# DeltaNet then Fourier mixing on one core: V scaled a step sooner, query products moved into the series, and the first two tiles of the second sample put in program order on all engines

## The chip, the cores and the metric

The kernel runs on one core of one Trainium2 chip. The metric is the device time of one execution in microseconds (us), lower is better. A core has a matrix engine (PE, whose weight loads the profile lists apart as PEld), a vector engine (DVE), a scalar engine (ACT), a GpSimd engine (POOL), and SP, whose queue issues nearly all DMAs here. Each engine works through its own queue of instructions in order and waits on semaphores for the others.

## The reference

Two blocks follow each other. All arrays are float32 but the two weights, which numpy makes float64.

```python
# q, k, v: (4, 8, 768, 48); beta: (4, 8, 768)
k_n = k / (norm(k) + 1e-6)
for t in range(768):                       # state: (4, 8, 48, 48), from zero
    y[t] = q[t] @ state
    state += beta[t] * outer(k_n[t], v[t] - k_n[t] @ state)
x = y as (4, 768, 384)                     # heads side by side
u = x + real(fft(fft(x, axis=1), axis=2))
un = (u - mean(u)) / sqrt(var(u) + 1e-6)
out = u + relu(un @ w_ch1) @ w_ch2         # 384 -> 1536 -> 384
```

## The kernel before

**Tiles.** A tile ("load") is 128 tokens of one of the 4 samples, all 8 heads; there are 24, numbered g, six to a sample (`NL` = 6). A tile has two chunks of 64 tokens. Four tiles make a round r for one inversion (`RL` = 4), so tiles 6 and 7, the first two of the second sample, are the last of round 1, and tile 8 begins round 2.

**What is made ahead of a tile.** `pre_a` turns K with PE (line 113, evicted by ACT at line 320) and makes the Gram products. `invert16(r)` inverts the diagonal blocks of a round with some 60 small DVE instructions, handed out in 46 steps: a transposition of G (line 475), a square root on ACT (481), eleven steps on norms, 30 steps of forward substitution (517 and 520), and two transpositions back (523, 526). `pre_q` turns Q (line 538, evicted at 320), multiplies it with K (548) and masks the product on DVE (555). `pre_m16(g)` joins the blocks of the inverse: Z on ACT (608), a product and its evictions (614, 617, 624), three products in a row evicted at 645 (DVE), 647 (ACT) and 649 (DVE), and V scaled by the norms (629), on DVE for the tiles before 8. For the first sample it also makes W and U (668, 670, evicted at 671 and 672). Each `yield` in such a generator ends a step, and the main program hands the steps out one by one.

**The recurrence.** `step(g, c)` carries the state over one chunk: a product with the state, a subtraction on DVE (720 for the first sample, 698 after it), for later samples a product with the inverse evicted on ACT (708), a product with K and an addition to the state (737 or 739). `outputs(g)` makes two products, evicted at 762 and 772/774.

**Weights.** The float64 weights come as pairs of int32 and are converted to float32 by `weight`, piece by piece, 12 pieces for each weight. One piece costs three ACT instructions (277, 278, 285) and five on DVE (286, 288, then 292, 295, 299). The generator of it, `conv`, gives two steps a piece: the second half of one piece, and the first half of the next. Line 256 then issues the DMA of a later piece.

**Stages.** The first sample's recurrence is the "series", a loop over g (lines 1175 to 1253). Then come the folds and sums of the Fourier block, then the loop over `KF` = 12 chunks of the first MLP with keys of tiles 9 to 11, `pre_m16(7)` and `conv` between them (lines 1301 to 1307). Then `period(g, side)` follows for every tile from 6 on. It has six slots (the loop at line 1059); each slot hands out pieces of the recurrence, of the inversion `inv`, of `conv` (tile 6 only), and of the MLP of the sample before (`side`): turned activations (`ptr`, evicted at 922), `ph` products evicted into hT at 936, and `po` products.

**Order.** Within `tc.manual_schedule(engines=...)` the engines named issue in the order of the program text; the order of the other engines is chosen by the framework's scheduler. Before the change there are three such regions: the first, up to line 1312, for PE, DVE, ACT and POOL; the second (1313 to 1316: the rest of `pre_q(6)`, and tiles 6 and 7) for PE alone; the third, from tile 8 on, for the four engines again. In the second region the scheduler places what DVE, ACT and POOL do, also among instructions of its neighbours. SP's order is the scheduler's everywhere.

**Buffers.** PSUM has three tags with two buffers each: `pair` (state products, query products, W), `one` (turned tiles, products of `pre_m16`, V with the inverse) and `post` (`ph`, `ptr`, `po`). A product waits until the buffer of the last but one of its tag was read.

Of the kernel before, what the change touches and what calls it, by code (L numbers as in the profile page):

```python
# [20 lines left out]
RL = 4  # L21
# [43 lines left out]
def kernel(  # L65
# [14 lines left out]
    NL = S // L  # L80
# [517 lines left out]
    def pre_m16(g):  # L598


        r, li = divmod(g, RL)
        K, GU = Ks[g % 3], GXs.pop((g, 16))
        MTd, Md, nT = rounds[r]
        m8 = slice(8 * li, 8 * li + 8)
        tags = ("QT", "LQ") if g < 2 * RL else ("WT", "WT")
        Z = wk.tile([128, 8, 2, W], F32, tag=tags[0], bufs=2, name="Z")
        for e in range(2):
            nc.scalar.activation(Z[:, :, e, :], Md[:, m8, :], ACT.Copy, scale=m_blk[:, e:e + 1])
        if g != 2 * RL:
            yield  # L610
        px = ps_one()
        for m in range(8):
            for hh in range(2):
                mm(px[full[hh], C * m:C * m + C], GU[full[hh], m, :],
                   Z[full[hh], m].rearrange("p b t -> p (b t)"), m == 0)
        ND2 = wk.tile([128, 8, C], F32, tag=tags[1], bufs=2, name="ND")
        nc.scalar.activation(ND2.rearrange("p m t -> p (m t)"), px, ACT.Copy)
        MT = wk.tile([128, 8, 2, W], F32, tag="MT", bufs=2, name="MT")
        for e in range(2):
            if g == 0:  # L620
                nc.vector.tensor_scalar(MT[:, :, e, :], MTd[:, m8, :], m_blk[:, e:e + 1], None,
                                        op0=ALU.mult)
            else:
                nc.scalar.activation(MT[:, :, e, :], MTd[:, m8, :], ACT.Copy,  # L624
                                     scale=m_blk[:, e:e + 1])

        def scaled_v():
            V = Vs.pop(g)
            (nc.vector if g < 2 * RL else nc.gpsimd).tensor_tensor(
                V.rearrange("p c j d -> p (c j) d"), V.rearrange("p c j d -> p (c j) d"),  # L630
                nT[:, m8, None].broadcast_to([128, 8, D]), op=ALU.mult)
            return V

        V = None if g else scaled_v()
        flat = "p m b t -> p (m b t)"
        yield
        for i in range(3):
            pz = ps_one()
            src = Z if i == 1 else MT
            for m in range(8):  # L640
                for hh in range(2):
                    mm(pz[full[hh], C * m:C * m + C], ND2[full[hh], m, :],
                       src[full[hh], m].rearrange("p b t -> p (b t)"), m == 0)
            if i == 0:
                nc.vector.tensor_tensor(Z.rearrange(flat), MT.rearrange(flat), pz, op=ALU.subtract)  # L645
            elif i == 1:
                nc.scalar.activation(MT.rearrange(flat), pz, ACT.Copy)  # L647
            else:
                nc.vector.tensor_tensor(MT.rearrange(flat), Z.rearrange(flat), pz, op=ALU.add)
            if i < 2 or g < 2 * RL:  # L650
                yield
        V = V or scaled_v()
        if g >= NL:
            pre[g] = (K, MT, V)
            yield
            return
        yield
        WT = wk.tile([128, 2, 2, 2, C], F32, tag="WT", bufs=2, name="WT")
        U0 = wk.tile([128, 2, 4, D], F32, tag="U0", bufs=2, name="U0")
        pw = ps_pair()  # L660
        pu = ps_one()
        for c in range(2):
            for j in range(4):
                for hh in range(2):
                    mt = MT[full[hh], 4 * c + j].rearrange("p b t -> p (b t)")
                    jj, jp = divmod(j, 2)
                    o = (2 * c + jj) * C
                    mm(pw[full[jp], hh, o:o + C], K[full[hh], 4 * c + j, :], mt, c == 0 and jj == 0)
                    o = (4 * c + j) * D
                    mm(pu[full[hh], o:o + D], mt, V[full[hh], c, j, :], c == 0 and j == 0)  # L670
        nc.scalar.activation(U0.rearrange("p c j d -> p (c j d)"), pu[:, 0:8 * D], ACT.Copy)
        nc.scalar.activation(WT.rearrange("p h c j t -> p h (c j t)"), pw[:, :, 0:4 * C],
                             ACT.Copy)
        pre[g] = (K, WT)
        Us[g] = U0
        yield
# [333 lines left out]
    def period(g, side):  # L1010
# [48 lines left out]
        for i in range(SLOTS):  # L1059
            if i == (2 if r + 1 < R16 else 3) and fresh and inv:  # L1060
                drain(inv)
                inv = None
            for p in pieces[i]:
                advance(p)
            if i == 5 and n + 1 == NL:
                o = outputs(g)
                drain(o)
                late = None
            if li == 1 and i == 1 and r > 1 and not last_round:
                inv = invert(r + 1)  # L1070
            if g == NL:
                advance(inv, 5)
                advance(conv, 2 if i < 5 else 4)
            elif inv:
                advance(inv, 8 if r + 1 < R16 else 6)
            if n + 2 >= NL and 0 < i < 5:

                if n + 2 == NL and i == 1:
                    fold = folds(b)
                advance(fold, 2)  # L1080
            at = SLOTS * n + i + 1
            if b > 1:
                want = 2 + (PIECES - KEEP - 2) * at // (SLOTS * NL)
            else:

                want = 2 + KF + (2 + 2 * KF) * at // (2 * SLOTS)
                if n > 1:
                    want = 4 + 3 * KF + (PIECES - KEEP - 4 - 3 * KF) * (at - 2 * SLOTS) // (
                        SLOTS * (NL - 2))
            for p in behind[i]:  # L1090
                advance(p)
            advance(side, want - done)
            done = max(want, done)
        load_v(g + 2)

    engines = {mybir.EngineType.PE, mybir.EngineType.DVE, mybir.EngineType.Activation,
               mybir.EngineType.Pool}
    with tc.manual_schedule(engines=engines):
# [76 lines left out]
        for g in range(NL - 1):  # L1175
# [4 lines left out]
            if g == 0:  # L1180
                advance(c0)
                fill(5)
                advance(nm)
                advance(n2)
                advance(c1)
                fill(5)
                advance(nm)
                advance(n2)
                advance(c1)
                fill(5)  # L1190
                advance(nm)
                advance(n2)
                drain(nm)
                advance(n2)
                drain(qs[1])
                advance(qs[2])
                advance(ms[3])
            else:
                advance(c0)
                if g == 2:  # L1200
                    advance(n2)
                else:
                    fill(5)
                if g > 2:
                    convert(1)
                advance(nm)
                advance(late)
                advance(c0)

                fill(5)  # L1210
                if g == 2:
                    convert(1)
                advance(n2)
                drain(late)
                if g == 4:
                    fold = folds(0)
                    fd = part(fold, 8)
                    advance(keys[0])
                advance(nm)
                advance(c1)  # L1220
                fill(4 if g == 1 else 3)
                if g > 1 and g != 4:
                    convert(2)
                drain(nm)
                advance(n2)
                advance(c1)
                if g == 4:
                    convert(2)
                    advance(n2)
                    drain(qs[g + 1])  # L1230
                    convert(1)
                else:
                    fill(1)
                    if g > 1:
                        convert(1)
                    advance(n2)
                    if g > 1:
                        convert(g - 1)
                    drain(qs[g + 1])
                if g + 2 < NL:  # L1240
                    advance(qs[g + 2])
                if g > 1 and g < 4:
                    advance(ms[g + 3])
            late = outputs(g)
# [10 lines left out]
        g = NL - 1  # L1255
# [54 lines left out]
            drain(m)  # L1310
        done = 3 + KF
        inv = invert16(2)
    with tc.manual_schedule(engines={mybir.EngineType.PE}):
        drain(nq)
        for g in range(NL, NL + 2):
            period(g, side)
    with tc.manual_schedule(engines=engines):
        for b in range(1, B):
            for g in range(max(NL * b, NL + 2), NL * (b + 1)):
                period(g, side)  # L1320

            advance(side, KEEP - 12)
# [42 lines left out]
```

## Time and profile before

| | |
|---|---|
| times of three runs | 743.04 us median, 741.8 to 745.75 |
| the profiled execution | 743.66 us, of which the span is 741.9 us |
| PE busy | 689.6 us, 93% of the span |
| DVE busy | 377.1 us, 51% |
| ACT busy | 262.5 us, 35% |
| POOL busy | 79.1 us, 11% |
| mean granted clock of PE | 0.972 |

Start times below are microseconds from the start of the span. The stages lie as follows: the series from about 40 to 113, the Fourier block to about 128, the first MLP loop from there to 160, tiles 6 and 7 from 160 to about 217. A line of the timeline reads: start, duration of the run of equal instructions, engine, source line, operation, what it writes and reads, count, and in brackets how long the engine was idle before it and what ended that. The products in float32 are recorded as two instructions each, so "x6" of `ph` is one chunk of three products.

### The profile page before, as it was taken

To read this page: it belongs to the slowest core of one execution; us is meant where nothing else is said; L and a number is where in the kernel's file an instruction comes from. 1 tells how busy PE (TensorE), PEld (TensorE's weight loads), DVE (VectorE), ACT (ScalarE), POOL (GpSimd) and SP (SyncE) were. 2 spreads that over 40 slices of the span, in tenths; PEclk is the share of its full clock that TensorE was granted. 3 is DMA by queue.
4 is the path that set the end of the run, shared out by engine and by line. 5 is a ranking of instruction groups with operands and counts; after the bars stand their busy time and mean duration, and the time that the engine had idled before them with its cause. 6 is when DMAs were issued, how large, how long until landed. Compare 5 with 4: busy or idle time off the path is not lost.

```text
span 741.9 us, 23087 instructions
## 1 busy us (share of the span) xinstructions
PE 689.6 (93%) x10176; PEld 529.3 (71%) x10176; DVE 377.1 (51%) x957; ACT 262.5 (35%) x641; POOL 79.1 (11%) x138
## 2 busy tenths in 40 slices
PE   6878789969999978999999999999999999999998
PEld 5667777757667656878768778777677687777684
DVE  5877787798711996170596328288212241600000
ACT  4534774787324212234323243133223121221120
POOL 8000001110000102031101120030112100200000
PEclk8699999988999999999999999999999999999999
DMA  9842452153124211003212211001110000000000
GB/s 153 221 72 43 98 140 87 24 138 99 28 51 83 46 34 28 1 11 72 41 39 50 45 40 28 11 23 37 43 34 13 12 12 5 18 1 21 11 11 21
DMA packets 108791, 36.10 MB, mean 49 GB/s; under 512 B 101873, under 2 KB 105234, under 8 KB 108690
## 3 DMA queue, kind: packets, MB, share of 16 engines
q1 hardware_dynamic: 106866, 33.86, 21.1%
q8 instruction: 80, 1.31, 0.8%
q0 software_dynamic: 640, 0.43, 0.4%
q10 hardware_dynamic: 1184, 0.33, 0.3%
q14 instruction: 21, 0.17, 0.1%
HBM read 29.88 MB, written 4.72 MB: 47 GB/s over the span
## 4 chain that ended last, share of the span: by engine, by line
PE 75%; DVE 15%; ACT 6%; issue 2%; DMA 1%; DVEq 0%; ACTq 0%
PE po L110 24%; PE ph L110 21%; PE one L110 15%; PE pair L110 9%; PE one L113 2%; DVE M L450 1%; DVE tmp L446 1%; PE ptr L113 1%; PE unread L1111 1%; DVE tmp L517 1%; DVE M L520 1%; DMA C<-in_k_dram 1%; DVE Z L645 1%; DVE S L739 1%; DVE w L292 1%
## 5 line engine op out<-in xcount | busy, mean ns | idle before, releaser
L110 PE MATMUL po<-w,hT 128*128 128x384 f32 x576 | 204.8, 495 | 0.0
L110 PE MATMUL ph<-unT,w 128*128 128x256 f32 x828 | 197.2, 390 | 0.0
L110 PEld LDWEIGHTS ph<-unT,w 128*128 128x128 f32 x828 | 155.1, 193 | 23.2
L110 PEld LDWEIGHTS po<-w,hT 128*128 128x128 f32 x576 | 103.5, 190 | 56.4
L936 ACT ACTIVATE hT<-ph 128x256 f32<-128x256 f32 x138 | 52.8, 383 | 144.2 <-PE ph L110 143.3
L951 DVE TENSOR_TENSOR x<-x,po 128x384 f32<-128x384 f32 x24 | 13.2, 551 | 107.0 <-PE po L110 107.0
L739 DVE TENSOR_TENSOR S<-S,pair 128x192 f32<-128x192 f32 x40 | 14.0, 351 | 71.2 <-PE pair L110 71.1
L110 PEld LDWEIGHTS one<-V,MT 64*64 64x64 f32 x768 | 31.1, 143 | 20.0 <-issue 7.7
L882 DVE TENSOR_TENSOR x<-x,one 128x193 f32<-128x193 f32 x24 | 8.5, 355 | 66.5 <-ACT Q L873 66.5
L110 PE MATMUL one<-V,MT 64*64 64x48 f32 x768 | 36.4, 230 | 4.2 <-DVE V L698 2.6
L450 DVE TENSOR_TENSOR M<-M,tmp 128x31 f32<-128x31 f32 (+15 forms) x93 | 34.5, 371 | 3.2
L446 DVE TENSOR_TENSOR tmp<-A,M 128x31 f32<-128x31 f32 (+15 forms) x93 | 34.1, 366 | 2.5
L698 DVE TENSOR_TENSOR V<-V,pair 128x192 f32<-128x192 f32 x33 | 11.5, 349 | 37.6 <-PE pair L110 31.4
L110 PE MATMUL one<-MT,ND 64*64 64x64 f32 x768 | 28.9, 225 | 1.1 <-ACT MT L647 0.7
L110 PEld LDWEIGHTS one<-dtab,F 97*128 97x128 f32 (+1 forms) x192 | 25.1, 191 | 6.4 <-ACT KT L320 1.3
L894 POOL TENSOR_SCALAR rstd<-mv 128x1 f32<-128x1 f32 x24 | 6.6, 276 | 216.4 <-DVE mv L890 216.4
L110 PEld LDWEIGHTS one<-MT,ND 64*64 64x64 f32 x768 | 26.5, 141 | 2.3 <-ACT MT L624 1.1
L320 ACT ACTIVATE QT<-one 128x512 f32<-128x512 f32 x24 | 14.3, 595 | 38.7 <-PE one L113 38.6
L110 PE MATMUL one<-dtab,F 97*128 97x97 f32 (+1 forms) x192 | 26.0, 275 | 0.9 <-ACT KT L320 0.9
L566 POOL TENSOR_TENSOR MT<-A,pack 128x512 f32<-128x512 f32 x12 | 12.8, 1067 | 130.3 <-PE one L110 64.8
L110 PEld LDWEIGHTS pair<-U,K 64*64 64x64 f32 x704 | 15.5, 134 | 15.5 <-issue 13.2
L110 PEld LDWEIGHTS pair<-S,KT 48*64 48x64 f32 x528 | 10.7, 133 | 21.7 <-issue 10.9
(181 smaller groups left out, 1029.4 us busy)
## 6 DMA issues: line engine op xcount, KB each, us to landing
w<-in_moe_w_ch_dram SPq DMA_DIRECT2D x12, 384.0 KB, 7.2
E<-in_moe_w_ch_dram SPq DMA_DIRECT2D x12, 384.0 KB, 3.8
out_dram<-x SPq DMA_DIRECT2D x24, 192.0 KB, 1.9
K<-in_k_dram SPq DMA_DIRECT2D x92, 48.0 KB, 2.3
V<-in_v_dram SPq DMA_DIRECT2D x92, 48.0 KB, 2.3
C<-in_k_dram SPq DMA_DIRECT2D x18, 192.0 KB, 9.5
Q<-in_q_dram SPq DMA_DIRECT2D x18, 192.0 KB, 3.4
w<-in_q_dram SPq DMA_DIRECT2D x6, 192.0 KB, 7.9
```

Of the source, the lines that this page charges most:

```text
L110: nc.tensor.matmul(o, lhsT=lhsT, rhs=rhs, start=start, stop=stop, skip_group_check=True)
L113: nc.tensor.matmul(o, lhsT=src, rhs=ident[0:src.shape[0], 0:src.shape[0]], is_transpose=True, start=start, stop=True, skip_group_check=True)
L292: nc.vector.tensor_tensor(pieces[i - lag][1].rearrange("p c f -> p (c f)"), man0, num0.bitcast(F32), op=ALU.mult)
L320: nc.scalar.activation(dst.rearrange("p h j t -> p (h j t)"), pt, ACT.Copy)
L446: nc.vector.tensor_tensor(t, A[:, j + 1:W, j:j + 1].broadcast_to([128, n, j + 1]), M[:, j:j + 1, 0:j + 1].broadcast_to([128, n, j + 1]), o ...
L450: nc.vector.tensor_tensor(M[:, j + 1:W, 0:j + 1], M[:, j + 1:W, 0:j + 1], t, op=ALU.add)
L566: nc.gpsimd.tensor_tensor(MT, MTd[:, m8, None, :].broadcast_to([128, 8, 2, W]), m_blk[:, None, :, None].broadcast_to([128, 8, 2, W]), op=A ...
L698: nc.vector.tensor_tensor(R4, R4, pw[:, :, 0:2 * D].rearrange("p a (j e) -> p a j e", e=D), op=ALU.subtract)
L739: nc.vector.tensor_tensor(s1v, s0.rearrange("p h j e -> p h (j e)"), pk, op=ALU.add)
L882: nc.vector.tensor_tensor(near, near, pb[:, 0, 0:MH + 1], op=ALU.add)
L936: nc.scalar.activation(hT[:, fc, :], ph, ACT.Relu)
L951: nc.vector.tensor_tensor(x[:, T, :], x[:, T, :], po, op=ALU.add)
```

## The change

Five edits are made together.

1. `pre_m16` hands out the scaling of V, for tiles below 8, in the step of the third product, ahead of the eviction at 649, instead of in the step after it.
2. In the series, for g from 1 to 4, the rest of `outputs` of the tile before (`late`) is begun ahead of `nm` instead of after it.
3. Also there, the second step of `pre_q(g + 1)` and the first of `pre_q(g + 2)` come ahead of the step of `n2` that makes its second product, instead of after it and after a piece of `conv`.
4. The first step of `invert16(2)` (the transposition at 475, the clearing of M on POOL) is handed out ahead of the rest of `pre_q(6)`, and in `period(6)` a slot hands out three steps of it at the old place and two at the slot's end; the slot's two (in the last slot four) halves of `conv` move to the slot's end as well, ahead of these two steps.
5. The second region goes: the rest of `pre_q(6)` joins the first region, and tiles 6 and 7 the third, which are both in program order on PE, DVE, ACT and POOL.

```diff
@@ pre_m16
+            if i == 2 and V is None and g < 2 * RL:
+                V = scaled_v()
             if i == 0:
                 nc.vector.tensor_tensor(Z.rearrange(flat), MT.rearrange(flat), pz, op=ALU.subtract)
...
             if i < 2 or g < 2 * RL:
                 yield
-        V = V or scaled_v()
+        if V is None:
+            V = scaled_v()
@@ period
             if g == NL:
-                advance(inv, 5)
-                advance(conv, 2 if i < 5 else 4)
+                advance(inv, 3)
             elif inv:
                 advance(inv, 8 if r + 1 < R16 else 6)
...
             advance(side, want - done)
             done = max(want, done)
+            if g == NL:
+                advance(conv, 2 if i < 5 else 4)
+                advance(inv, 2)
         load_v(g + 2)
@@ the series
                 if g > 2:
                     convert(1)
+                advance(late)
                 advance(nm)
-                advance(late)
                 advance(c0)
...
                 if g == 4:
                     convert(2)
+                    drain(qs[g + 1])
                     advance(n2)
-                    drain(qs[g + 1])
                     convert(1)
                 else:
                     fill(1)
                     if g > 1:
                         convert(1)
+                    drain(qs[g + 1])
+                    advance(qs[g + 2])
                     advance(n2)
                     if g > 1:
                         convert(g - 1)
-                    drain(qs[g + 1])
-                if g + 2 < NL:
-                    advance(qs[g + 2])
                 if g > 1 and g < 4:
                     advance(ms[g + 3])
@@ the end of the first region, and the regions after it
         inv = invert16(2)
-    with tc.manual_schedule(engines={mybir.EngineType.PE}):
+        advance(inv)
         drain(nq)
-        for g in range(NL, NL + 2):
-            period(g, side)
-    with tc.manual_schedule(engines=engines):
         for b in range(1, B):
-            for g in range(max(NL * b, NL + 2), NL * (b + 1)):
+            for g in range(NL * b, NL * (b + 1)):
                 period(g, side)
```

## The prediction

> **What bounds the kernel now.** The page first: PE is busy for nearly the whole span, so a change counts only where PE waits or runs at a lower clock.
>
> ```profile
> PE 689.6 (93%) x10176; PEld 529.3 (71%) x10176; DVE 377.1 (51%) x957; ACT 262.5 (35%) x641; POOL 79.1 (11%) x138
> ...
> PEclk8699999988999999999999999999999999999999
> ```
>
> The second line shows the granted clock below full at the start, near slices 9 and 10, and nowhere later by much. Then the stages around tiles 6 and 7, in stretches of 10 us (duration; busy PE, PEld, DVE, ACT, POOL; clock; DMA):
>
> ```profile
> 150.00:160.00 10.00, 9.02 (x106) 7.09 (x104) 9.54 (x28) 9.78 (x24) 1.55 (x3) 1.00 0.75 187
> 160.00:170.00 10.00, 5.31 (x30) 3.93 (x29) 9.42 (x23) 7.62 (x19) 1.32 (x3) 0.60 0.41 110
> 170.00:180.00 10.00, 9.49 (x96) 7.33 (x94) 8.55 (x30) 7.41 (x18) 0.00 (x0) 0.89 0.41 130
> ```
>
> Here DVE is full and PE half empty: `conv` and the inversion set the pace. Clocks of 0.60 and 0.89 fit half speed from 161.9 to 172.2. PE's own timeline shows the hole:
>
> ```profile
> 159.46 0.65 PE L113 MATMUL one<-pack,Q 128*128 128x128 f32 x4
> 164.22 0.90 PE L113 MATMUL ptr<-pack,un 128*128 128x128 f32 x3 [4.11 <-ACT hT L936]
> 165.71 0.90 PE L113 MATMUL ptr<-pack,un 128*128 128x128 f32 x3 [0.58 <-ACT unT L922]
> ...
> 167.56 5.12 PE L110 MATMUL ph<-unT,w 128*128 128x256 f32 x12
> ```
>
> The `ptr` turns wait for a `post` buffer that ACT reads at 936. The twelve `ph` after them took 5.12 us, against 2.86 at full clock. ACT's timeline tells why it read late:
>
> ```profile
> 161.57 0.63 ACT L278 ACTIVATE O<-O,edges 128x384 int32<-128x384 int32 x1
> 162.84 0.26 ACT L481 ACTIVATE nrm<-A 128x32 f32<-128x32 f32 x1 [0.65 <-DVE A L475]
> 163.35 0.55 ACT L285 ACTIVATE O<-E 128x384 f32<-128x384 uint32 x1 [0.25 <-DVE w L292]
> 163.80 0.37 ACT L936 ACTIVATE hT<-ph 128x256 f32<-128x256 f32 x1
> ```
>
> The scheduler put the inversion's square root ahead of hT; it waited for the transposition on DVE (1.91 us at 160.90). In the series, the lines of PE that the other edits concern:
>
> ```profile
> 53.44 0.22 PE L110 MATMUL one<-V,MT 64*64 64x48 f32 x1 [0.86 <-issue]
> ...
> 67.88 1.05 PE L110 MATMUL one<-Z,ND 64*64 64x64 f32 x29 [0.72 <-DVE Z L645]
> ...
> 81.10 1.05 PE L110 MATMUL one<-Z,ND 64*64 64x64 f32 x29 [0.72 <-DVE Z L645]
> ...
> 85.91 1.05 PE L110 MATMUL one<-Z,GU 64*64 64x64 f32 x29 [0.60 <-ACT Z L608]
> ...
> 92.14 1.05 PE L110 MATMUL one<-Z,ND 64*64 64x64 f32 x29 [0.65 <-DVE Z L645]
> ...
> 96.95 1.05 PE L110 MATMUL one<-Z,GU 64*64 64x64 f32 x29 [0.51 <-ACT Z L608]
> ```
>
> **What the Trainium skill says.** "TensorE: Matmul & The Clock Gate", Part 1, states that PE falls to half clock after an idle window of about 3.4 us, and rises after one busy window, the windows running free. The trace agrees in kind: 161.9 to 172.2 is three such windows. It differs in strictness: the window before 161.9 was about half busy (PE stopped at 160.1). The same page, under its detail on the array, calls ACT's and DVE's queues strict FIFO; hT, whose product ended by 158.9, stood until 163.80 behind three unrelated instructions.
>
> **The series (edits 1 to 3).** No instruction is added or removed. Upper bound: the waits above vanish, 0.86 + 0.72 + 0.72 + 0.65 + 0.60 + 0.51 = 4.1 us, and 0.50 before the W products at 88.25, 4.6 us. I walked each period, with these durations, along DVE's queue:
> - g = 0: V (0.55, a pitch of 0.47) goes ahead of 649 at 51.52. The W products start when 649 ends, near 52.66, instead of when V ends, 53.34: gain 0.78.
> - g = 1: V stands before 649 while DVE is full with `fill`; 772 and 774, which free the W products' `pair` buffer (PE idle 60.75 to 62.73), come 0.4 later: gain left 0.4. Then the query products fill the 0.72 before Z,ND. But S,QT, moved ahead of MT,ND on PE, takes the `pair` buffer that 555 must read, and 555 stands behind the 2.1 us transposition (523): to 70.15. MT,ND and what follows wait for it: gain left 0.
> - g = 2: V falls into DVE's 0.56 idle ahead of 649: 0.3 gained. The next S,QT again waits for 555.
> - g = 3: with V gone from between 772 and 720, and 555 ahead of `conv`, W starts near 87.4 instead of 88.4, and Z,GU of the next period near 95.6 instead of 96.95.
> - g = 4: 720 near 98.3 instead of 99.61; what is late next is W's eviction on ACT.
> Sum at the end of the series: 1.6 gained, from -0.9 (the blocked S,QT costs more) to 4.6. From 105 to 119 DVE's chain of folds sets the time; it starts from the series' last state, so the gain passes through. V of tile 6 adds 0.47 ahead of the last fold, hidden behind PE's sums (those of O are wanted at 119.84, its last fold ends at 118.3). The V loads are covered: V of tile 5 is issued by 82.9, takes 2.6 us to land (median), and is wanted near 95.8.
>
> In the MLP loop, V of tile 7 moves from 148.71 to before 649 at 144.63. It delays 286 at 147.39, on which ACT waits (277 at 147.78) before an unbroken run to 160.7: 0.4 lost.
>
> **Tiles 6 and 7 (edits 4 and 5).** PE's order is the same; nothing is added. In the times of the old trace:
> - DVE. The transposition now stands behind all that the MLP loop emits. After 889 (from 159.83, as 555 of tile 6 no longer precedes it) come 890 and three times a second and a first half of a piece, 1.5 + 0.53 us each: 160.4 + 6.1 = 166.5. The transposition ends at 168.3 instead of 162.7.
> - ACT. hT of chunk 10 comes at 162.1 (behind 285), that of chunk 11 at 164.0; good, the two `ptr` can run at 162.5 and 164.5. But the order is then: the loop's last halves (to 166.0), the square root, the turned Q (320), the two `unT` (922). The root waits for the transposition: 168.4 to 168.6; 320 to 169.1; both `unT` to 169.9. Behind the root are queued all of these, and PE waits for `unT`.
> - PE. `ph` begins at 170.0 instead of 167.56: 2.4 lost. PE idles from about 166.4 on, so the clock is half again; it rises only after a full window. Counting 3.4 to 6.8 us of half clock from the first `ph`, 5.1 in the middle, costs 2.6 against 2.3 now: 0.3 lost.
> - Rest of tile 6. DVE needs about 3 us a slot (a piece's 2.03, five steps of 0.1 to 0.3), PE 2.86 to 3.5: PE leads, and the wait of 0.76 at 180.25 for 698 goes: 0.8 gained.
> - Tile 7. Its first slot has 13 substitution steps and both transpositions left: from 698, 2.4 + 1.3 + 3.9. Then 739, 772, 774 and only then Z at 608 (two of 0.45), which the scheduler had put at 195.05, ahead of 774. Z,GU comes 0.9 later against the tile's begin.
> Sum: 0.4 + 2.4 + 0.3 - 0.8 + 0.9 = 3.2 lost. Bounds: if `unT` is ready as now, 0.6 is gained at most from these waits with the clock as it is; at worst one more half window (1.7) and a late piece (2.0) come on top, 6.9 lost. SP's order isn't fixed by the change: its K, V and beta loads in tile 6 are issued long before their use, and cost nothing unless they stand before a weight piece. POOL's clearing of M moves behind the last `rstd` (163.0), hidden until 508 (178.9).
>
> **The sum.** 743.66 (the profiled execution: 741.9 of span and 1.8 around it) - 1.6 + 3.2 = 745.3. The median of the runs is 0.6 lower, so 744.7. Afterwards PE is the bound to the end, and the inversion from 241 to 287 starts from PE's own order, so the difference carries through.
>
> **The rivals.**
> - *Slower (0.33).* The last halves in the MLP loop starve: weight piece 7 is issued by SP behind K loads. It must be out 3.8 us (the median landing) before 166.5, by 162.7; four K loads of 0.65 in front would put it 2.0 late, with the transposition, root and `unT` in a row behind it, and PE one more half window (1.7): 748.4. For it: pieces 10 and 11 stood behind two K loads at 173.10. Against: piece 7 had a free queue at 164.45.
> - *Faster (0.13).* The old hole of 4.11 was the scheduler's doing, and no new one comes, because DVE gets through its halves sooner. Bounded by DVE, which was idle only 0.29 + 0.58 + 1.45 = 2.3 us from 158 to 175: with the series' 1.6, and 0.5 for the clock, 738.6. Against: the order of ACT in the program text.
> - *The series gives nothing (0.12)*: S,QT blocked by 555 eats it; 3.2 lost, 746.2.
>
> **How the numbers follow.** The forecast has 0.42, its own range 742 to 747. A measurement of this kernel tells 0.5%, 3.7 us, from no change: 739.3 to 746.8 is the same. Slower: 0.31 of the slower rival, 0.05 of the last, 0.04 of the forecast's tail, 0.40. Faster: 0.09 and 0.02, 0.11. The rest, 0.49, is the same. Leaving out half the faster rival and the far end of the slower one, the range is 740.3 to 750.
>
> **What would show it.** In the changed profile: the square root (481) right behind the transposition (475), that behind the loop's last 288, `unT` behind both; PE idle ahead of `ph`, not ahead of the first `ptr`; no wait of Z,ND for 645 in the series for g of 1 to 3, and S,QT waiting for 555; V,MT without a wait. I am wrong if `unT` comes before the root, or the stretch from 113 to 200 gets shorter than before.

## The result

The changed kernel takes 748.69 us (median of four runs, 748.19 to 749.21); the kernel before, on the same chip, 743.16 us. The ratio is 1.0061, with a 95% interval of 1.0037 to 1.0085: slower, by some 4.5 us if the ratio is taken. The profiled execution took 748.19 us (span 746.4) against 743.66 (741.9). So the time lies in the range given, and four us above the likeliest case: a loss of 1.6 us against the median before was forecast, and the loss is 4.5.

The new page differs little in its sums. In the clock row, the fourth and the sixteenth slice are lower than before; neither lies in tiles 6 and 7, which are in slices 9 to 12. A slice is 18.7 us long, so a single stretch of half clock of 3.4 us leaves it at 0.91 and does not show.

```profile
PE 689.9 (92%) x10176; PEld 529.7 (71%) x10176; DVE 379.8 (51%) x957; ACT 262.3 (35%) x641; POOL 79.6 (11%) x138
...
PEclk8798999988999998999999999999999999999999
```

To find the place, both traces were cut at instructions that occur in both. Times of the stages in us (the marks are starts):

| stage | before | after | difference |
|---|---|---|---|
| start of the program to the first copy of the state | 45.18 | 43.74 | -1.44 |
| series, folds, to the first Fourier sum | 67.40 | 67.55 | +0.15 |
| Fourier sums, to the first `unT` | 16.01 | 15.48 | -0.53 |
| MLP loop and the turn to tile 6, to the first `ph` in tile 6 | 38.97 | 43.08 | +4.11 |
| tile 6, to the first `po` | 22.71 | 21.18 | -1.53 |
| tile 7, to the eviction at 645 for tile 8 | 12.65 | 15.42 | +2.77 |
| the rest | 538.96 | 539.94 | +0.98 |

No edit touches the first row: it is before all of them. In the last, 0.71 falls between the fourth inversion's transposition (405) and the 120th record of `po`, where one stretch of half clock (near 289) lasts 6.8 us instead of 3.4. The change shows in the three rows from 4 to 6: 74.33 us became 79.68, 5.35 more.

PE's timeline after has the hole in its new place:

```profile
158.18 0.65 PE L113 MATMUL one<-pack,Q 128*128 128x128 f32 x4
161.31 0.55 PE L113 MATMUL ptr<-pack,un 128*128 128x128 f32 x3 [2.48 <-ACT hT L939]
164.11 0.90 PE L113 MATMUL ptr<-pack,un 128*128 128x128 f32 x3 [2.25 <-ACT hT L939]
164.94 1.09 PE L110 MATMUL one<-V,MT 64*64 64x48 f32 x16
169.85 4.42 PE L110 MATMUL ph<-unT,w 128*128 128x256 f32 x12 [3.82 <-ACT unT L925]
...
199.45 1.26 PE L110 MATMUL one<-Z,GU 64*64 64x64 f32 x32 [1.30 <-ACT Z L608]
200.64 3.74 PE L110 MATMUL po<-w,hT 128*128 128x384 f32 x6
```

The old wait of 4.11 for hT at the first `ptr` has become three, of 2.48, 2.25 and 3.82. The `po` at 200.64 run at half clock: the first six take 3.74 us, all eight 4.38. Before, Z,GU had followed without a wait, and the eight `po` took 2.85:

```profile
197.08 0.69 PE L110 MATMUL pair<-QT,KT 48*64 48x64 f32 x32 [0.67 <-DVE S L739]
197.59 1.11 PE L110 MATMUL one<-Z,GU 64*64 64x64 f32 x32
198.64 2.85 PE L110 MATMUL po<-w,hT 128*128 128x384 f32 x8
```

ACT's timeline tells why `unT` is late:

```profile
165.32 0.54 ACT L285 ACTIVATE O<-E 128x384 f32<-128x384 uint32 x1
...
168.29 0.26 ACT L481 ACTIVATE nrm<-A 128x32 f32<-128x32 f32 x1 [2.44 <-DVE A L475]
168.46 0.58 ACT L320 ACTIVATE QT<-one 128x512 f32<-128x512 f32 x1
168.94 0.86 ACT L925 ACTIVATE unT<-ptr 128x384 f32<-128x384 f32 x2
...
198.42 0.89 ACT L608 ACTIVATE Z<-G,pack 128x256 f32<-128x256 f32 x2
```

The square root (481) waits 2.44 us for the transposition, with 320 and both `unT` in a row behind it. The stretches of 10 us (busy PE, PEld, DVE, ACT, POOL; clock; DMA):

```profile
160.00:170.00 10.00, 2.62 (x23) 1.90 (x23) 9.86 (x20) 6.58 (x15) 1.80 (x3) 0.64 0.49 140
170.00:180.00 10.00, 10.00 (x96) 8.07 (x97) 9.60 (x32) 6.31 (x15) 0.00 (x0) 0.85 0.30 89
200.00:210.00 10.00, 10.00 (x162) 6.86 (x158) 2.38 (x5) 2.32 (x6) 0.00 (x0) 0.83 0.01 3
```

From 160 to 170 PE does 2.62 us of work, where it was 5.31, and DVE is full with 9.86. From 200 to 210 the clock is 0.83.

### The profile page after: what moved, and what is told of

It is laid out like the page before. It is cut to its first block, busy times and chain, and to the rows that moved or that the text cites. A ratio compares the mean times of both kernels' runs of the same rounds, so it can differ in the third digit from the quotient of the medians.

```text
span 746.4 us, 23084 instructions
## 1 busy us (share of the span) xinstructions
PE 689.9 (92%) x10176; PEld 529.7 (71%) x10176; DVE 379.8 (51%) x957; ACT 262.3 (35%) x641; POOL 79.6 (11%) x138
## 4 chain that ended last, share of the span: by engine, by line
PE 76%; DVE 14%; ACT 6%; issue 2%; DMA 1%; DVEq 0%; ACTq 0%; POOL 0%; POOLq 0%
PE po L110 24%; PE ph L110 23%; PE one L110 14%; PE pair L110 9%; PE one L113 2%; DVE M L450 1%; DVE tmp L446 1%; PE ptr L113 1%; PE unread L1116 1%; DMA C<-in_k_dram 1%; ACT wtmp L285 1%; PE pf L110 1%; DVE G L523 1%; ACT wtmp L277 1%; DVE O L299 1%
```

## The experiments

Ratios are against the kernel before on the same chip, with 95% intervals. "The three rows" means the stages from the first `unT` to tile 8's eviction at 645, together 74.33 us before and 79.68 after.

**Each half of the change alone.** `e1_series` keeps edits 1 to 3 and takes 4 and 5 back; `e2_regions` keeps 4 and 5 and takes 1 to 3 back.

> Edits 1 to 3 alone (V sooner, outputs and query products inside the series); tiles 6 and 7 as before, left to the scheduler. My theory (the loss lies in tiles 6 and 7, the series gives little): 741.5 to 744.5, within 0.3% of before; from the first state to the first Fourier sum 66 to 68 us (67.4 before, 67.55 after); the hole of 4.1 us ahead of the first turned activations stays. Rival (the blocked S,QT and the moved V slow the kernel down by themselves): 746 or more.

> Edits 4 and 5 alone (tiles 6 and 7 in program order on all engines, the third inversion's first step placed), the series as before. My theory: nearly the whole loss, 747 to 749; a hole of 3.5 us or more ahead of the ph products of tile 6, Z,GU of tile 8 waiting for 608 in tile 7, and a half clock window behind that. Rival (the loss needs the series' edits too): below 745.

Measured: `e1_series` 743.28 us, 0.9989 (0.9973 to 1.0005); `e2_regions` 748.45 us, 1.0070 (1.0046 to 1.0094), its three rows 78.84 us. The whole loss is in edits 4 and 5, and the series' edits are worth nothing that can be measured. One thing expected of `e2_regions` did not come in its profile: Z,GU of tile 8 waits for 608 as in the changed kernel, but no half clock follows.

```profile
201.73 1.15 PE L110 MATMUL one<-Z,GU 64*64 64x64 f32 x32 [1.30 <-ACT Z L608]
202.81 2.52 PE L110 MATMUL po<-w,hT 128*128 128x384 f32 x7
```

Its stage of tile 7 takes 13.77 us, against 15.42. The three rows are long all the same, since half clock lasts 13.7 us around the first `ph` here, and 10.2 in the changed kernel.

**The square root out of `unT`'s way.** In the changed kernel, the five steps of the inversion in tile 6's first slot all go to the slot's end:

```diff
-                advance(inv, 3)
+                advance(inv, 3 if i else 0)
...
-                advance(inv, 2)
+                advance(inv, 2 if i else 5)
```

> The changed kernel with one thing moved: in the first slot of tile 6 all five steps of the inversion come at the slot's end, so that on ACT the square root stands behind the turned Q, both unT and a half piece of conv. My theory (unT is held by the root, the root by the transposition): unT 2.5 to 4 us earlier, the hole ahead of ph 1 us or less, 744 to 746.5. Rival (DVE's amount of work sets the pace, whatever stands where): the wait comes back in tile 7, ahead of Z,GU of tile 8, and the time stays within 1 us of 748.

Measured: 748.6 us, 1.0074 (1.0047 to 1.0101). PE's timeline of it:

```profile
169.13 4.91 PE L110 MATMUL ph<-unT,w 128*128 128x256 f32 x12 [1.46 <-ACT unT L925]
182.12 0.67 PE L110 MATMUL one<-V,MT 64*64 64x48 f32 x16 [1.26 <-DVE V L701]
199.39 0.69 PE L110 MATMUL pair<-QT,KT 48*64 48x64 f32 x32 [1.12 <-DVE S L742]
201.38 1.98 PE L110 MATMUL one<-Z,GU 64*64 64x64 f32 x32 [1.30 <-ACT Z L608]
```

The hole ahead of `ph` fell from 3.82 to 1.46, and the row up to it from 43.08 to 40.32, as the theory of the blocked root has it. But the time did not follow: tile 6's row grew from 21.18 to 23.00, with a wait for DVE (1.26 for 701), and tile 7's from 15.42 to 17.48, with another (1.12 for 742). Of these last 2.06 us some 1.7 are the clock, at half speed for 6.8 us from 200.6 instead of for 3.4, so the 80.80 us of the three rows overstate what DVE cost. DVE itself got through no sooner: from the first `unT` of the MLP loop to the end of 526 it is 70.34 us here, and 70.45 in the changed kernel, and Z,GU of tile 8 starts after 72.57 and 72.68. The theory fell as the whole story, and its rival held: the work that PE no longer waits for is still to be done by DVE, which had no wait left to give up.

**Z of tile 8 ahead of the outputs.** In the changed kernel, the step of `pre_m16(8)` with Z (608) becomes one of its own, and is handed out before the evictions at 772 and 774, not after them. PE's order stays.

```diff
-        if g != 2 * RL:
-            yield
+        yield
         px = ps_one()
...
+                if fresh:
+                    pieces[2].insert(1, pm)
                 for i in range(4):
```

> The changed kernel with one thing moved: in tile 7's third slot, Z of tile 8 (608) is a step of its own, handed out behind the state's addition and ahead of the second half of outputs (772, 774); PE's order is the same. My theory: the wait of Z,GU (1.3 us after) falls below 0.5, and with it the half clock window that begins near 200: 2 to 3 us gained, 745.5 to 747. Rival (Z,GU is held by 739 and the transpositions, not by ACT's order; the half clock has another cause): less than 0.7 us gained.

Measured: 745.76 us, 1.0018 (1.0003 to 1.0034). The products of Z follow their predecessors in PE's timeline without a wait, and the clock stays full:

```profile
199.67 0.69 PE L110 MATMUL pair<-QT,KT 48*64 48x64 f32 x32 [0.31 <-DVE S L741]
200.19 1.11 PE L110 MATMUL one<-Z,GU 64*64 64x64 f32 x32
201.23 2.85 PE L110 MATMUL po<-w,hT 128*128 128x384 f32 x8
```

The stage of tile 7 went from 15.42 to 12.29 us. Of the 3.13, the wait itself is 1.30, and the half clock that is gone about 1.7 (half of the 3.4 us that it lasted). `e2_regions`, with the wait and without the half clock, lies between: 13.77, which is 1.48 above `e4_z`. So the wait of 1.3 us cost more than twice its length in the changed kernel's profile, and about its length where no half clock came behind it. The ratios, 1.0018 against 1.0061, tell of some 3 us too.

**The inversion between the instructions of `conv`.** On top of `e4_z`, in tile 6, one step of the inversion goes after each DVE instruction of a piece (after 286, 288, 292, 295 and 299), until the slot's five are spent, in place of three before and two after. The call of `tick` stands after each of the five:

```diff
+    def tick():
+        if quota[0]:
+            quota[0] -= 1
+            advance(inv)
...
+                tick()
...
+                quota[0] = 5
                 advance(conv, 2 if i < 5 else 4)
-                advance(inv, 2)
+                advance(inv, quota[0])
+                quota[0] = 0
```

> The kernel with Z placed first in tile 7 (e4_z), with the inversion's five steps of each slot of tile 6 put between the five DVE instructions of conv instead of three ahead and two behind; the root thereby stands behind unT, as in e3_root. My theory (a DVE instruction that needs the one just before it costs some 0.1 us more than when another stands between; the scheduler's order had mixed them): from the first ph of tile 6 to the eviction at 645 of tile 8 2 to 4 us shorter than the 33.6 us of e4_z plus what the root's place moves out of the stretch ahead; mean pitch at 517 back near 0.22 us from 0.32; 742 to 744.5. Rival (the pitch is the same in any order; DVE's sum of work decides): within 0.7 us of e4_z's 745.8, with the hole moved as in e3_root.

Measured: 744.06 us, 0.9997 (0.9975 to 1.0019); the three rows 75.12 us. The row to the first `ph` is 40.36 instead of 43.08, since 320 and both `unT` now stand ahead of the root (the two `unT` at 166.43, the root at 168.51). And DVE became shorter with the same 77 instructions: from 475 to the end of 526 it needs 29.5 us, of which 1.06 are waits (of over 0.1 us), against 30.9 with 0.12 of such waits in the changed kernel. In the whole time, 0.9997 against the 1.0018 of `e4_z`, the gain is not clear of the noise. Two expectations were missed. From the first `ph` to 645 it takes 34.77 us, 1.5 less than the 33.56 of `e4_z` and the 2.72 by which the row ahead shrank, added together; 2 to 4 had been expected. And the mean pitch at 517 (from its start to that of the next instruction) is 0.30 us, not 0.22; one of the fifteen holds a wait for PE of 0.93, and the mean of the others is 0.23. DVE's timelines, of the changed kernel first:

```profile
179.88 0.22 DVE L517 TENSOR_TENSOR tmp<-A,M 128x56 f32<-128x56 f32 x1
180.13 0.22 DVE L520 TENSOR_TENSOR M<-M,tmp 128x56 f32<-128x56 f32 x1
180.38 0.24 DVE L517 TENSOR_TENSOR tmp<-A,M 128x78 f32<-128x78 f32 x1
...
181.01 0.55 DVE L295 SCALAR_TENSOR_TENSOR O<-w,O 128x384 f32<-128x384 int32 x1
181.60 0.56 DVE L299 SCALAR_TENSOR_TENSOR O<-E,O 128x384 int32<-128x384 int32 x1
```

and of this one (its lines 305, 310, 529 and 532 are 295, 299, 517 and 520 there):

```profile
178.90 0.22 DVE L529 TENSOR_TENSOR tmp<-A,M 128x56 f32<-128x56 f32 x1
179.03 0.56 DVE L305 SCALAR_TENSOR_TENSOR O<-w,O 128x384 f32<-128x384 int32 x1
179.50 0.22 DVE L532 TENSOR_TENSOR M<-M,tmp 128x56 f32<-128x56 f32 x1
179.62 0.56 DVE L310 SCALAR_TENSOR_TENSOR O<-E,O 128x384 int32<-128x384 int32 x1
```

Where the next instruction reads what the last one wrote, it starts 0.25 us after a 517 of 56 columns and 0.59 after a 295; where another stands between, the next starts after 0.13 and 0.47. The durations are the same. It is so in all fourteen traces (from 155 to 200 us): behind such a 517, 0.24 or 0.25 us in 18 cases where the next needs it, and 0.13 in 10 where not; behind a 295, 0.58 or 0.59 in 63, and 0.41 to 0.48 in 62. Before the change the scheduler had mixed them:

```profile
180.69 0.21 DVE L517 TENSOR_TENSOR tmp<-A,M 128x56 f32<-128x56 f32 x1
180.82 0.55 DVE L295 SCALAR_TENSOR_TENSOR O<-w,O 128x384 f32<-128x384 int32 x1
181.29 0.21 DVE L520 TENSOR_TENSOR M<-M,tmp 128x56 f32<-128x56 f32 x1
181.42 0.55 DVE L299 SCALAR_TENSOR_TENSOR O<-E,O 128x384 int32<-128x384 int32 x1
```

**What brings half clock near 108.** In the changed kernel, as in `e1_series`, PE runs at half clock for 3.4 us from about 108; not so before, nor in `e2_regions`. `e6_g4` is `e1_series` with the old order of the queries' products for g = 4; `e7_v` is edit 1 alone.

> Edits 1 to 3 alone (e1_series), but for g = 4 the step of n2 ahead of the query product, as in the kernel before. My theory: the half clock window near 108, which every kernel with the series' edits shows and neither without them, comes from the new wait of QT,KT for 278 (1.07 us after) and the ones behind it in g = 4; it goes, and 0.8 to 1.7 us with it: 741.5 to 742.8. Rival (the window comes from the earlier holes or from chance): as e1_series, 743.3.

> Edit 1 alone (V scaled sooner), all else as before. My theory: the waits of V,MT go (0.86 us at 53.44), 0.5 us is lost in the MLP loop for tile 7's V; 743 to 744.5, the stretch from the first state to the first Fourier sum 0.5 to 1.2 us shorter than 67.4, the next to the first unT the same. Rival (V is what blocks 772 and costs the series): over 745.

Measured: `e6_g4` 743.67 us, 0.9991 (0.9973 to 1.0010), with 6.8 us of half clock from 106: the guess that g = 4 brings it failed. `e7_v` 744.1 us, 0.9990 (0.9970 to 1.0009), with none there.

**All the cures together.** `e8_all` is the changed kernel with Z first, the woven inversion, the old order for g = 4, and V of tile 7 at its old, later step (`g < 2 * RL - 1` in edit 1's condition). `e9_noq` is that without edits 2 and 3. `e8b_all` is `e8_all` again, beside `e9_noq` on one chip.

> The changed kernel with all that helps: Z first and the woven inversion (e5_weave), the old order for g = 4 (e6_g4), and tile 7's V scaled late, as before. My theory: 740 to 742.5, faster than before and than e1_series. Rival (program order costs in tiles 6 and 7 whatever the order): 743.5 or more.

> As e8_all, but without edits 2 and 3 (outputs and query products stand where they stood before). My theory: what edits 2 and 3 save in PE waits they give back in the half clock window that all seven kernels with them show between 105 and 112 and none of the three without; so no such window here, and a time within 1.5 us of e8b_all. Rival A (edits 2 and 3 are worth their 1 to 2 us): 1.5 us or more slower than e8b_all. Rival B (they cost): 1.5 us or more faster.

> The kernel of e8_all once more, beside e9_noq on one chip. My theory: again faster than before, ratio 0.996 to 0.999; the half clock window between 105 and 112 is there again. Rival (the 0.9974 was luck of the clock's phase): ratio 0.9995 or more.

Measured: `e8_all` 741.65 us, 0.9974 (0.9960 to 0.9989), and again 742.47, 0.9977 (0.9959 to 0.9995); `e9_noq` 742.9, 0.9980 (0.9964 to 0.9996). So there is a version that beats the kernel before, by 0.2 to 0.3%. Edits 2 and 3 make no difference to it: 0.4 us, less than the intervals. The row to `ph` is 39.84 with V of tile 7 late, 40.36 with it early (`e5_weave`).

**The clearing of M, and edit 2.** `e10_clear` is `e8_all` with the inversion's first step split: POOL's clearing of M (474) goes to chunk 5 of the MLP loop, the transposition stays.

```diff
+            if fc == 5:
+                inv = invert16(2)
+                advance(inv)
...
-        inv = invert16(2)
         advance(inv)
```

`e11_late` is `e9_noq` with edit 2.

> The version with Z first, the inversion woven into conv, the old order of g = 4 and tile 7's V late, and besides POOL's clearing of M moved back, from beside conv's tail at 161 to an earlier chunk of the MLP loop. Mine: DVE's 286 at the end of the MLP loop falls from 1.20 back to about 0.35 us, ACT's 277 no longer waits 0.8 for it, and the time from the first unT to the first ph of tile 6 falls by about 0.8 us, from 39.8 to 39.0; ratio between 0.995 and 0.998. Rival: the clearing makes another DVE instruction of the loop pay the same 0.8 us, and the stage keeps its 39.8.

> The same version without edit 3, and with edit 2 alone in the series (the rest of outputs begun ahead of nm). If edit 2 brings the stretch of half clock between 105 and 112, the clock of 104 to 112 is below 0.95 here; if edit 3 does, it is 1.00, as in the four kernels without either. The time tells little: ratio between 0.996 and 1.000 in both cases.

Measured: `e10_clear` 742.43 us, 0.9981 (0.9965 to 0.9997). DVE's timeline of it, at the place where the changed kernel's 286 took 1.20 us (293 is that line here):

```profile
162.10 0.56 DVE L310 SCALAR_TENSOR_TENSOR O<-E,O 128x384 int32<-128x384 int32 x1
162.57 0.35 DVE L293 TENSOR_SCALAR O<-E 128x384 int32<-128x384 int32 x1
162.84 0.35 DVE L296 TENSOR_SCALAR w<-E 128x384 int32<-128x384 int32 x1
```

The row to `ph` fell from 39.84 to 39.25, 0.6 of the 0.8 expected; in the whole time that can't be seen. `e11_late`: 745.1 us, 1.0010 (0.9992 to 1.0028), above the 0.996 to 1.000 expected: edit 2 without edit 3 looks worse than both or neither, but its interval overlaps a little with that of `e10_clear`, from the same chip, so this stays open. Its clock over 104 to 112, with that of `e9_noq`, which differs in edit 2 alone (busy PE, PEld, DVE, ACT, POOL; clock; DMA), is

```profile
104.00:112.00 8.00, 7.05 (x227) 6.29 (x228) 7.26 (x21) 4.55 (x12) 0.00 (x0) 0.79 0.36 84
```

for `e11_late`, and for `e9_noq`

```profile
104.00:112.00 8.00, 6.01 (x268) 5.10 (x260) 7.29 (x20) 5.78 (x14) 0.00 (x0) 1.00 0.42 95
```

So edit 2 is enough to bring the half clock near 108, as far as one profile of each kernel can tell. A stretch that lies there, begun between 100 and 111, is in all ten profiles of kernels with edit 2, and in none of the four without (the kernel before, `e2_regions`, `e7_v`, `e9_noq`). Which of its waits trips it stays open.

## Why the prediction was right and wrong

The forecast for tiles 6 and 7, with V of tile 7, was +3.2 us; the three rows show +5.35:

| term of the sum | forecast | measured | from |
|---|---|---|---|
| V of tile 7 in the MLP loop | +0.4 | +0.5 | `e5_weave` against `e8_all`, row to `ph` |
| root, 320, `unT` behind the transposition | +2.4 | +2.8 | the changed kernel against `e3_root`, row to `ph` (43.08 to 40.32) |
| POOL's clearing of M | 0 | +0.6 | `e8_all` against `e10_clear`, row to `ph` |
| clock of the first twelve `ph` | +0.3 | -0.7 | 5.12 us before, 4.42 after |
| wait of 0.76 for 698 | -0.8 | -0.8 | gone in the timeline after |
| Z of tile 8 behind 774 | +0.9 | +3.1 | `e4_z` against the changed kernel, stage of tile 7 |

The measured column adds to 5.5. Most terms are differences between kernels that are alike in the rest, from one profile each, so each is good to a few tenths at best.

**Right: the order on ACT.** The root stood behind the transposition and ahead of 320 and both `unT`; the first `ph` was forecast at 170.0 and came at 169.85. The two `ptr` ran at 161.31 and 164.11, for which "good, the two `ptr` can run at 162.5 and 164.5" had been written, and no longer wait for the root. And the price of that order alone is the 2.8. But `e3_root` shows that it was not to be had back by undoing the order: see the next point.

**Right in the sum, wrong in the reason: "PE leads" in the rest of tile 6.** PE has no wait from the first `ph` to 197.2, and the 0.8 came. But I had DVE at 3 us a slot, from durations alone; it took 3.7 (six pieces begin, at 292, from 169.22 to 187.71), the recurrence's instructions among them. It ran from 166.36 to 197.22 with 0.12 us of waits, where it had waited 2.0 in that stretch before. So PE led only because it had begun late. The fifteen pairs of 517 and 520 took 8.60 us instead of 6.79, start to start. Some 0.5 of that is one 517 that took 0.88 us, not 0.29, beside POOL's 629. The rest is the order: program order put them in rows, each reading what the one before wrote, while the scheduler had spread the first seven pairs between `conv` and the recurrence. `e3_root` shows what a full DVE means: there the hole ahead of `ph` shrank by 2.4 us, and waits for DVE of 1.26 and 1.12 took its place.

**Mis-sized: Z,GU.** Z late behind 774 was the mechanism, and the wait 1.30 us, near the 0.9. What the term left out is the clock: with the wait came 3.4 us of half speed at 200.4, some 1.7 us, and `e2_regions`, without it, agrees (13.77 against 15.42 for the stage). The Trainium skill, "TensorE: Matmul & The Clock Gate", Part 1, gives the window of about 3.4 us and lets it run free, and asks for an idle window; here the waits ahead of 200.4 are 0.29 and 1.30 us, so again less than a whole window was idle. I priced this risk for the slower bound alone.

**Wrong: the clearing "hidden until 508".** POOL had the time, but DVE paid. In the changed kernel DVE's 286 took 1.20 us beside POOL's clearing, and ACT's 277 waited for it (the timeline of all engines):

```profile
160.85 1.20 DVE L286 TENSOR_SCALAR O<-E 128x384 int32<-128x384 int32 x1
160.86 0.97 POOL L474 MEMSET M<- 128x1056 f32 x1
...
162.08 0.62 ACT L277 ACTIVATE O<-O,edges 128x384 int32<-128x384 int32 x1 [0.82 <-DVE O L286]
```

**Wrong: the series' 1.6.** The local waits went as forecast: V,MT starts without one at 51.41 (0.86 before), Z,ND without one, and S,QT waits for 555, by 0.33 and 0.65. PE's timeline after:

```profile
67.59 1.08 PE L110 MATMUL one<-Z,ND 64*64 64x64 f32 x29
69.29 0.68 PE L110 MATMUL pair<-S,QT 48*64 48x48 f32 x32 [0.33 <-DVE LQ L555]
```

From the state's first copy to the first `unT`, 0.38 us is left of it. The half clock near 108 takes 1.7 (half of 3.4); the earlier stretches of the series add up to 6.8 us in both. That this is where the gain went is an estimate, for no run has edits 2 and 3 without that stretch. `e1_series` and `e7_v`, with the series' edits and with edit 1 alone, find nothing in the whole time. "The series gives nothing" was a rival, but for another reason (555 ahead of S,QT). The slower rival, the starved weight piece, didn't happen: the transposition ran at 166.36, with 166.5 forecast for no starving.

**Luck.** The measured 748.69 lies next to that rival's 748.4, and the range reached so far up for its sake. It came by other ways: the gain of the series was lost and the wait of Z,GU cost three times its price, 1.2 and 2.2 us worse than forecast, and the clearing 0.6.

## What to carry to other kernels

When an order is moved from a scheduler into the program text, look not only at what is queued behind a wait but at how the instructions lie on the full engine: rows of small ones, each reading the one before, cost here up to 0.12 us apiece more than the same ones woven into independent work. Price a new wait of PE with the clock in mind, since one of 1.3 us cost 3.1 in one profile and 1.5 in another, with and without half clock behind it. And a hole that closes on PE brings nothing while another engine works without a gap up to the next product that needs it.

## What the runs showed of the hardware

- *A VectorE instruction behind its own producer.* It starts about 0.12 us later than one that reads something else: 0.25 against 0.13 after a 517 of 56 columns, 0.59 against 0.47 after a 295. The Trainium skill, "VectorE: DVE Perf Modes", "The DRAIN you can't avoid", says that a semaphore after each of eight copies, of some 1.7 us each, cost nothing extra against one after the last. Here the instruction that needs the one before it does pay, the 0.12 us. Whether the wait for its producer's semaphore or the dependence itself takes them, no run here tells apart.
- *The shared port.* Beside POOL's clearing (0.97 us), DVE's 286 took 1.20 us, not 0.35, in every kernel with edit 4 that leaves the clearing there. The Trainium skill, "SBUF — State Buffer", "SBUF: two separate sides", says that VectorE's instructions in a two-port mode and GpSimd's exclude each other for a whole instruction, and that those with two SBUF inputs only mind a GpSimd instruction that reads. The traces agree: 286 has one input, and its 0.35 us against the 0.55 of 292, of the same size, fits such a mode, though no run shows the mode itself. Moved to 146.07 in `e10_clear`, the clearing, which reads nothing, lay beside instructions with two inputs, which kept their 0.55 us. And beside POOL's 629, which does read (0.83 us at 186.81 in the changed kernel), DVE's 517 with its two inputs took 0.88 us, not 0.29.
- *Half clock in a busy stretch.* It came near 108 and 200 in the changed kernel with PE idle for 1.1 and 1.6 us of the 3.4 before it. In the fourteen traces, from 40 us on to 5 us before the end, it began 64 times, each time behind 3.41 us of which PE had been idle 0.94 to 3.35; other such stretches, with up to 1.99 us idle, had full clock behind them, so the idle time alone does not decide. It ended 64 times, each time behind 3.41 us with at most 0.32 idle. And it moves from one kernel to the next that hardly differs: the row from the state's first copy to the first Fourier sum was 64.96 us in `e7_v`, with no such stretch, and 69.01 in `e10_clear`, with one of 3.4 and one of 13.7 us that began at 100.7. Profiled executions can be compared to about a microsecond or two for that reason, unless their stretches of half clock are counted.
